# An output stage's half-size products 2 and 4 made of seven small products each, with shared sums on GpSimd and the row sums of q moved

## The chip, the cores and the metric

One core of one Trainium2 chip runs the kernel. The metric is the device time of one execution in microseconds, lower is better. The time before is 257.67 us, the median of 3 runs (257.42 to 258.0).

## The reference

Linear attention over 8 batches of 8 heads, 576 rows and 64 columns, then a two-layer network with an exact GELU over all 4608 rows.

```python
def _attn_ref(q, k, v):
    q_s = exp(q - max(q, -1)); q_s = q_s / (sum(q_s, -1) + 1e-09)
    k_s = exp(k - max(k, 2));  k_s = k_s / (sum(k_s, 2) + 1e-09)
    kv = einsum('bhsd,bhse->bhde', k_s, v)
    return einsum('bhsd,bhde->bhse', q_s, kv)
# x = attn_out as (4608, 512); w_in (512, 2048); w_out (2048, 512)
h = x @ w_in
g = 0.5 * h * (1.0 + erf(h / sqrt(2)))
return g @ w_out
```

## The kernel before, in words

The rows are handled in nine **chunks**: chunk c = 0 to 7 is 512 rows of batch c, chunk 8 is the 64 rows that each batch has left over. Every chunk goes through four stages. The attention of a batch b is `exp_q` and `exp_k` on ScalarE (ACT), row sums and reciprocal of q on VectorE (DVE; `q_sums`, lines 258 to 264), the scaling of q on GpSimd (POOL; `q_scale_parts`, line 278, eight pieces of 128x256), a cast of v on POOL (line 190), a transposing DMA of q issued by SyncE (SP; `xbar_step`, line 333), the small products k by v on TensorE (PE; `kv_mm`, line 225) and their normalization on DVE (`kv_norm`, lines 245 and 246). The x stage (`x_all`, lines 353, 380 and 378) makes the transposed attention output: eight products of 64x512, four copies out of PSUM, two by ACT and two by DVE.

The two large products use a **seven-product scheme** (Winograd's form of Strassen) on 2x2 blocks, from chunk 2 on in both. In the h stage (`h_waves`, x by w_in) the products are `mm(1..7, q)` at line 498, each quarter q four matmuls of 128x256. Sums of x blocks come from `x_sums` (DVE, line 430); products are summed in PSUM and with DVE adds `e_sum` and `r_sum`, and GELU is by ACT (line 522). `mm(7, 0)` writes a bank that `e_sum(0)` reads, so it waits for that sum; `mm(4, q)` waits for `r_sum(q)`. `s_parts` (DVE, line 430) makes the sums of g that the output stage needs.

In the y stage (`y_phase`, g by w_out) each of the seven half-size products is sixteen matmuls of 128x256 at line 686: two row blocks j, eight k tiles. Their order is 1, 5, 6, 2, 7, 3, 4. Between them stand the hooks `after(i)`, to which the loop at lines 1060 to 1078 hangs the attention of batch nb = c + 2: exp_q after product 1, exp_k and the cast of v after 5, row sums and scaling of q and the next loads after 6, and, after 3, `next_x`: the x stage of chunk c + 1, the transposing DMA of q, the k by v products of batch nb (nb below 8 only) and the first x sums. So product 4 of y stands on PE behind the x stage and the k by v products, and ahead of the h stage of the next chunk.

The order of the work is written out by hand: each engine takes its instructions in the order of the program text, waits are for semaphores, and PSUM's eight banks are handed round by the table `roles`. Before the cast of v a one-element POOL copy (`touch_s`, line 1047) waits for the last DVE sum of g.

Of the kernel before, what the change touches and what calls it, by code (L numbers as in the profile page):

```python
# [16 lines left out]
def kernel(  # L17
# [11 lines left out]
    nc = tc.nc  # L29
# [78 lines left out]
    def v_buf(b):  # L108

        i = b % 2 if b < 4 else 0  # L110
        return f32in.tile([128, HP, NS * D], FP32, tag=f"vf{i}", name="f", bufs=1)

    def load_pair(b, name, t, parts=1):
        f = v_buf(b) if name == "v" else f32in.tile([128, HP, NS * D], FP32, tag=name + "f")
        st[b][name + "f"] = f
        src = t[b].rearrange("h (p n) d -> (h p) (n d)", n=NS).rearrange("(x q) f -> q x f", q=128)
        n = HP // parts
        for i in range(parts):
            h0 = i * n
            if b == 0 and name == "k" and i == 0:  # L120

                nc.scalar.dma_start(out=f[:, 0, :], in_=src[:, 0, :])
                h0 = 1
            nc.sync.dma_start(out=f[:, h0:(i + 1) * n, :], in_=src[:, h0:(i + 1) * n, :])

    def load_k1(i):

        if i == 0:
            st[1]["kf"] = f32in.tile([128, HP, NS * D], FP32, tag="kf", name="f")
        src = k[1].rearrange("h (p n) d -> (h p) (n d)", n=NS).rearrange("(x q) f -> q x f", q=128)  # L130
        nc.sync.dma_start(out=st[1]["kf"][:, 2 * i:2 * i + 2, :], in_=src[:, 2 * i:2 * i + 2, :])

    def load_v1(i):

        if i == 0:
            st[1]["vf"] = v_buf(1)
# [321 lines left out]
    def turn_roles():  # L458
# [2 lines left out]
        roles.update(bb=r["x3"], ba=r["kv1"], x0=r["bb"], x1=r["kv0"], x2=r["x0"], x3=r["ba"],  # L461
                     kv0=r["x1"], kv1=r["x2"])

    def h_waves(c, mid):


# [45 lines left out]
        def e_sum(q):  # L512
            tt(held["B", q], held["A", q], held["r", q])
# [4 lines left out]
        def gelu(kind, *qs):  # L518
            up, half = {"C": (1, lo), "B": (1, hi), "A": (0, lo), "r": (0, hi)}[kind]
            for q in qs:  # L520
                t = 2 * q + (0 if up else HK)
                nc.scalar.activation(out=g[:, t:t + 2, half], in_=held[kind, q], func=AF.Gelu)  # L522

        vcopy, scopy = nc.vector.tensor_copy, nc.scalar.copy
        mm(1, 0, 1)
        seed(0)
        if mid:
            seed(1)
            mm(1, 2, 3)
# [36 lines left out]
        else:  # L566
            mm(5, 0, 1)
            seed(1)
            p5_copy(0, scopy)
            p5_copy(1, scopy)  # L570
            mm(6, 0, 1)
            x_sums(c, (3,))
            e_sum(0)
            e_sum(1)
            x_sums(c, (4,))
            mm(2, 0, 1)
            gelu("C", 0, 1)
# [12 lines left out]
            seed(3)  # L590
            gelu("A", 0, 1)
            p5_copy(2, vcopy)
# [66 lines left out]
    def y_operands(c):  # L659
# [8 lines left out]
        }  # L668
        return act, wgt

    def y_phase(c, ins):
# [8 lines left out]
        def two(ps):  # L680
            return ps.rearrange("p (j n) -> p j n", j=2)

        def mm(m, ps, first):
            for j in range(2):
                for k in range(HK):
                    nc.tensor.matmul(  # L686
                        ps[:, j * HN:(j + 1) * HN], act[m][:, k, j * 128:(j + 1) * 128],
                        wgt[m][:, k, :], start=(first and k == 0 and j == 0),
                        stop=(k == HK - 1), skip_group_check=True,
                    )  # L690

        def after(i):
            for fn in ins.get(i, []):
                fn()

        mm(1, pa, True)
        (nc.vector.tensor_copy if c == 1 else nc.scalar.copy)(out=c11, in_=two(pa))
        after(1)
        mm(5, pb, True)
        nc.vector.tensor_copy(out=c22, in_=two(pb))  # L700
        after(5)
        mm(6, pa, False)
        tt(two(pb), two(pa), c22)
        after(6)
        mm(2, pc, True)
        tt(c11, c11, two(pc))
        after(2)
        mm(7, pa, False)
        tt(c22, two(pa), c22)
        after(7)  # L710
        mm(3, pb, False)
        nc.scalar.copy(out=c12, in_=two(pb))  # L712
        y_store(c, 0, ysb[0])
        after(3)
        mm(4, pa, False)
        nc.scalar.copy(out=c21, in_=two(pa))
        y_store(c, 1, ysb[1])
        after(4)

    def y_last(c):  # L720
# [26 lines left out]
        for j in range(2):  # L747
# [267 lines left out]
    for m in (3, 2, 4, 1):  # L1015
# [11 lines left out]

    y_phase(1, {
        1: [sums[3], lambda: norm_q(2, 0, 2)],
        6: [lambda: norm_q(2, 1, 2, nc.vector), lambda: cast_v_all(3), lambda: xbar_step(2), lambda: exp_q(3)],  # L1030
        2: [lambda: kv_step(2), lambda: exp_k(3)],
        7: [lambda: q_sums(3)],
        3: [lambda: table(AF.Gelu)],
# [8 lines left out]
        q_scale(3, nc.gpsimd)  # L1042
        xbar_step(3)

    def touch_s():

        nc.gpsimd.tensor_copy(out=scr[:, 2:3], in_=s12[:, HK - 1, HT:HT + 1])
# [61 lines left out]
```

## Time and profile before

| what | value |
|---|---|
| median of 3 runs | 257.67 us |
| profiled execution, its own time | 257.79 us |
| its span | 255.7 us |
| granted TensorE clock | 0.998 |
| PE busy | 248.6 us, 97% of the span |
| DVE busy, ACT busy | 189.8 us and 189.1 us, 74% each |
| POOL busy | 53.9 us, 21% |
| h stage of chunk 6 | 176.6 to 188.9 us, PE busy all of it |
| y stage of chunk 6 | 188.9 to 201.75 us, PE busy all of it |

The page is read from the shares of busy time to the chain of work that ended last, and then stage by stage in the timeline: for each engine a start, a duration, and in brackets the idle time before with what ended it. Durations of matmuls overlap, so the spacing of a group is its length less one duration, divided by one less than its count. Names in the timeline are output, arrow, inputs.

### The profile page before, as it was taken

How to read it: one execution, taken by the hardware profiler on the slowest of the kernel's cores; microseconds unless marked ns; L12 is line 12 of the kernel's file. 1: busy time of each engine (PE TensorE's matmuls, PEld its weight loads, DVE VectorE, ACT ScalarE, POOL GpSimd, SP SyncE). 2: the span in 40 equal slices, each digit the busy share in tenths (PEclk: the TensorE clock that was granted, in tenths of full speed). 3: DMA queues.
4: the chain of work that ended last, by engine and by line, in shares of the span. 5: the costliest groups of instructions: out<-in, count | busy, mean ns of one | idle time of the engine just before them, and what ended most of it. 6: DMA issues, size and time to landing. Idle time of an engine off the chain costs nothing.

```text
span 255.7 us, 6526 instructions
## 1 busy us (share of the span) xinstructions
PE 248.6 (97%) x2678; PEld 195.8 (77%) x2678; DVE 189.8 (74%) x337; ACT 189.1 (74%) x323; POOL 53.9 (21%) x85
## 2 busy tenths in 40 slices
PE   7899999999999999999999999999999999999993
PEld 3444444448888888888888888888888888888883
DVE  1878698877987985898589858985798689448931
ACT  4776878699887986899688968895887687068711
POOL 1530023000705065005500560056000700000000
PEclk9999999999999999999999999999999999999999
DMA  7999999994289997933693369203400240040033
GB/s 239 401 363 424 402 408 398 399 410 178 53 256 380 267 355 234 318 143 102 228 313 142 91 222 245 45 0 118 133 3 0 103 145 3 0 167 3 0 82 86
DMA packets 43166, 50.23 MB, mean 196 GB/s; under 512 B 20224, under 2 KB 30464, under 8 KB 42880
## 3 DMA queue, kind: packets, MB, share of 16 engines
q1 hardware_dynamic: 42416, 49.13, 56.5%
q10 hardware_dynamic: 720, 0.69, 1.1%
q8 instruction: 21, 0.34, 0.5%
q14 instruction: 9, 0.07, 0.1%
HBM read 36.70 MB, written 9.44 MB: 180 GB/s over the span
## 4 chain that ended last, share of the span: by engine, by line
PE 79%; DMA 16%; DVE 1%; issue 1%; ACT 1%; ACTq 0%; SPq 0%
PE ya L686 19%; PE qa L498 19%; PE yb L686 9%; PE qb L498 9%; DMA w<-in_moe_w_in_dram 6%; PE ps L387 6%; DMA f<-in_k_dram 5%; PE qc L498 5%; PE yc L686 5%; DMA f<-in_v_dram 3%; PE ya L739 2%; DMA touch<-in_moe_w_in_dram 2%; PE yb L739 1%; PE kv L225 1%; PE ps L353 1%; DVE s L430 1%
## 5 line engine op out<-in xcount | busy, mean ns | idle before, releaser
L498 PEld LDWEIGHTS <-quad_s 128*128 128x128 bf16 x448 | 43.8, 98 | 5.2
L686 PEld LDWEIGHTS <-g 128*128 128x128 bf16 x448 | 43.2, 98 | 6.0 <-issue 0.4
L686 PEld LDWEIGHTS <-s 128*128 128x128 bf16 x336 | 32.8, 98 | 4.2 <-DVE s L430 0.4
L498 PEld LDWEIGHTS <-wi_bf 128*128 128x128 bf16 x336 | 32.9, 98 | 4.0 <-issue 0.2
L278 POOL TENSOR_TENSOR e<-e,recq 128x256 bf16<-128x256 bf16 x40 | 24.2, 642 | 30.7 <-DVE recq L264 21.1
L498 PE MATMUL qa<-quad_t,quad_s 128*128 128x256 bf16 x224 | 29.2, 273 | 0.0
L430 DVE TENSOR_TENSOR qb<-qa,r 128x512 f32<-128x512 f32 x28 | 18.2, 695 | 14.2 <-PE qa L498 9.6
L387 PE MATMUL ps<-xT,wi_bf 128*128 128x512 bf16 x128 | 28.1, 379 | 0.2 <-ACT xT L380 0.2
L686 PE MATMUL yb<-wo_bf,s 128*128 128x256 bf16 x224 | 26.9, 273 | 0.1
L686 PE MATMUL ya<-w,g 128*128 128x256 bf16 x224 | 26.8, 273 | 0.0
L263 DVE TENSOR_REDUCE qsum<-e 128x16 f32<-128x1024 bf16 (+1 forms) x12 | 20.9, 1740 | 4.6 <-ACT e L173 4.5
L387 PEld LDWEIGHTS <-wi_bf 128*128 128x128 bf16 x128 | 12.4, 98 | 15.3 <-issue 0.7
L393 ACT ACTIVATE g<-ps 128x512 bf16<-128x512 f32 x32 | 17.6, 602 | 6.2 <-PE ps L387 5.8
L173 ACT ACTIVATE e<-f 128x512 bf16<-128x512 f32 (+1 forms) x42 | 20.5, 557 | 2.0 <-DMA f<-in_q_dram 1.9
L522 ACT ACTIVATE g<-r 128x512 bf16<-128x512 f32 x28 | 17.3, 631 | 6.1 <-DVE r L430 6.1
L522 ACT ACTIVATE g<-qc 128x512 bf16<-128x512 f32 x28 | 15.2, 594 | 7.5 <-PE qc L498 7.5
L269 POOL TENSOR_TENSOR e<-e,recq 128x1024 bf16<-128x1024 bf16 (+1 forms) x4 | 9.3, 2330 | 48.5 <-DVE recq L264 41.9
L430 DVE TENSOR_TENSOR r<-qa,r 128x512 f32<-128x512 f32 x28 | 18.0, 683 | 0.9 <-PE qa L498 0.7
L178 ACT ACTIVATE ek<-f 128x2304 bf16<-128x2304 f32 (+1 forms) x10 | 17.2, 1726 | 1.1 <-DMA f<-in_k_dram 1.1
L190 POOL CAST v_aug<-f 128x576 bf16<-128x576 f32 x25 | 17.0, 716 | 3.6 <-DMA f<-in_v_dram 3.5
L378 DVE CAST xT<-ps 128x512 bf16<-128x512 f32 x18 | 11.6, 682 | 8.0 <-PE ps L353 6.4
L712 ACT COPY y_sb<-yb 128x512 f32<-128x512 f32 x7 | 4.1, 585 | 17.2 <-PE yb L686 16.1
(96 smaller groups left out, 442.0 us busy)
## 6 DMA issues: line engine op xcount, KB each, us to landing
out_dram<-y_sb SPq DMA_DIRECT2D x16, 512.0 KB, 3.4
f<-in_k_dram SPq DMA_DIRECT2D x6, 1152.0 KB, 9.6
f<-in_v_dram SPq DMA_DIRECT2D x6, 1152.0 KB, 9.2
f<-in_q_dram SPq DMA_DIRECT2D x6, 1024.0 KB, 7.0
w<-in_moe_w_in_dram SPq DMA_DIRECT2D x6, 512.0 KB, 9.0
f<-in_v_dram SPq DMA_DIRECT2D x8, 288.0 KB, 6.5
f<-in_q_dram SPq DMA_DIRECT2D x4, 512.0 KB, 8.9
w<-in_moe_w_out_dram SPq DMA_DIRECT2D x2, 1024.0 KB, 11.5
```

The source lines that it names most:

```text
L173: nc.scalar.activation(out=dst[:, i], in_=src[:, u], func=AF.Exp)
L178: nc.scalar.activation(out=ek[b % 2][:, i:i + n], in_=st[b]["kf"][:, i:i + n].rearrange("p x (n d) -> p x n d", n=NS), func=AF.Exp,)
L190: eng.tensor_copy(out=o, in_=i)
L263: nc.vector.reduce_sum(out=qsum, in_=st[b]["eq"][:, :, i * w:(i + 1) * w, :], axis=AX.X)
L278: nc.gpsimd.tensor_tensor(out=e, in0=e, op=ALU.mult, in1=st[b]["recq"][:, j, i:i + 4].unsqueeze(2).to_broadcast([128, 4, D]),)
L378: nc.vector.tensor_copy(out=st[b]["xT"][:, hp, :], in_=ps)
L387: nc.tensor.matmul(ps, wi_bf[:, dm, t * 128:(t + 1) * 128], st[c]["xT"][:, dm, :], start=(dm == 0), stop=(dm == NDM - 1),)
L393: nc.scalar.activation(out=st[c]["g"][:, t, :], in_=ps, func=AF.Gelu)
L430: eng.tensor_tensor(out=out, in0=in0, in1=in1, op=op)
L498: nc.tensor.matmul(held[kind, q][:, u], w, mov[m][:, k], start=(m in (1, 5) and u == 0 and k == 0), stop=(k == 1), skip_group_check=True,)
L522: nc.scalar.activation(out=g[:, t:t + 2, half], in_=held[kind, q], func=AF.Gelu)
L686: nc.tensor.matmul(ps[:, j * HN:(j + 1) * HN], act[m][:, k, j * 128:(j + 1) * 128], wgt[m][:, k, :], start=(first and k == 0 and j == 0), ...
```

## The change

In chunks 2 to 7 the half-size products 2 and 4 of the y stage are each computed by a second level of the same scheme: seven **sets** of four matmuls of 128x128 in place of sixteen matmuls of 128x256. A class `Two` holds it. Its weight sums are made once, on POOL, in y of chunk 1 (`two_begin`, eight operations of 128x512). Its sums of g are made in every chunk on POOL (`inner(0)` and `inner(1)` in `h_waves`, eight operations of 128x256 each: s1, s2, s4, s3 for product 4, then the same for product 2). The results are gathered in a bank X (sets 2, 3, 4, 5 side by side) and a bank D (sets 1, 6, 7 on top of each other, read in between), and added to the output tile by DVE in five adds: a, b (128x128, from D), c (128x256, D read twice), d (128x128, from X), e (128x512, from X).

The PE order of y becomes 1, 5, 6; sets 1, 5, 2, 4, 6, 3 of product 2; 7; set 7 of product 2, set 1 of product 4; the first half of 3; sets 5, 2, 6; the second half of 3; sets 7, 3; `next_x`; set 4. The copy of the first part of c21 moves from behind product 4 to behind product 7.

The row sums of q (in two halves), reciprocal, scaling and transposing DMA move from y of chunk c for batch c + 2 into h of chunk c for batch c + 1 (`q_wide`; from chunk 3 on). `touch_s` is gone. k gets the same buffers as v: two up to batch 3, and one from batch 4 on. The two buffers that this frees hold the weight sums and the sums of g. In `y_last` one copy goes from ACT to DVE.

```diff
+    def q_wide(b):
+        qsum = small.tile([128, J, H], FP32, tag="qsum")
...
+        def part(j):
+            js = slice(2 * j, 2 * j + 2)
+            nc.vector.reduce_sum(out=qsum[:, js], in_=st[b]["eq"][:, js], axis=AX.X)
+        def rest():
+            nc.vector.reciprocal(st[b]["recq"], qsum)
+            q_scale_parts(b)
+            xbar_step(b)
...
+        def inner(a):
+            if c < B:
+                two[4].sums(c, a)
+                two[2].sums(c, a)
...
             gelu("A", 0, 1)
+            inner(0)
...
             x_sums(c, (3,))
+            q_ops = q_wide(c + 1) if c + 1 <= B else []
+            for fn in q_ops[0:1]:
+                fn()
             e_sum(0)
             e_sum(1)
...
             r_sum(0)
             r_sum(1)
+            for fn in q_ops[1:]:
+                fn()
...
         gelu("A", 2, 3)
+        inner(1)
...
+        def sums(self, c, a):
+            ks = slice(2 * a, 2 * a + 2)
+            (a11, a21), (a12, a22) = self.halves(y_operands(c)[0][self.m], ks)
+            s1, s2, s3, s4 = (self.s[:, i, ks] for i in range(4))
+            tt(s1, a21, a22, eng=nc.gpsimd)
+            for o, i0, i1 in ((s2, s1, a11), (s4, a12, s2), (s3, a11, a21)):
+                tt(o, i0, i1, ALU.subtract, eng=nc.gpsimd)
...
+                        1: (A[:, e, lo], W[:, e, lo], "D", 0),
+                        2: (A[:, o, lo], W[:, o, lo], "X", 0),
+                        3: (s[:, 3, i], W[:, o, hi], "X", 1),
+                        4: (A[:, o, hi], w[:, 3, i], "X", 2),
+                        5: (s[:, 0, i], w[:, 0, i], "X", 3),
+                        6: (s[:, 1, i], w[:, 1, i], "D", 0),
+                        7: (s[:, 2, i], w[:, 2, i], "D", 0),
...
+            t2.begin(c, pc, bank(roles["x1"], "yd"))
+            t2.mm(1, 5, 2, 4)
+            t2.add("a", c11)
+            t2.mm(6, 3)
+            t2.add("b", c11)
+            after(2)
+            mm(7, pa, False)
+            tt(c22, halves(pa), c22)
+            t2.mm(7)
+            after(7)
+            nc.scalar.copy(out=c21, in_=halves(pa))
+            t4.begin(c, bank(at["ya"], "yf"), bank(roles["kv1"], "ye"))
+            t4.mm(1)
+            t2.add("c", c11)
+            mm(3, pb, False, (0,))
+            t4.add("a", c21)
+            t2.add("de", c11)
+            t4.mm(5, 2, 6)
+            t4.add("b", c21)
+            mm(3, pb, False, (1,))
+            nc.scalar.copy(out=c12, in_=halves(pb))
+            y_store(c, 0, ysb[0])
+            t4.mm(7, 3)
+            t4.add("c", c21)
+            after(3)
+            t4.mm(4)
+            t4.add("de", c21)
...
-            nc.scalar.copy(out=c12, in_=pb)
+            (nc.vector.tensor_copy if j else nc.scalar.copy)(out=c12, in_=pb)
...
-            yi[6] = [lambda: q_sums(nb), lambda: q_scale_parts(nb)]
+            yi[6] = []
-            yi[5] = [lambda: exp_k(nb), touch_s, lambda: cast_v_all(nb)]
+            yi[5] = [lambda: exp_k(nb), lambda: cast_v_all(nb)]
-        if nb <= B:
-            xbar_step(nb)
```

More of the change, by code (lines that the diff above doesn't have):

```diff
@@ L106, in load_main, with kv_buf @@
             nc.sync.dma_start(out=f[:, i * n:(i + 1) * n, :], in_=src[:, i * n:(i + 1) * n, :])
-    def v_buf(b):
+    def kv_buf(b, name):
         i = b % 2 if b < 4 else 0
-        return f32in.tile([128, HP, NS * D], FP32, tag=f"vf{i}", name="f", bufs=1)
+        return f32in.tile([128, HP, NS * D], FP32, tag=f"{name}f{i}", name="f", bufs=1)
     def load_pair(b, name, t, parts=1):
-        f = v_buf(b) if name == "v" else f32in.tile([128, HP, NS * D], FP32, tag=name + "f")
+        f = kv_buf(b, name)
         st[b][name + "f"] = f
@@ L128, in load_k1 @@
         if i == 0:
-            st[1]["kf"] = f32in.tile([128, HP, NS * D], FP32, tag="kf", name="f")
+            st[1]["kf"] = kv_buf(1, "k")
         src = k[1].rearrange("h (p n) d -> (h p) (n d)", n=NS).rearrange("(x q) f -> q x f", q=128)
@@ L462, in turn_roles @@
                      kv0=r["x1"], kv1=r["x2"])
+    def q_wide(b):
+        qsum = small.tile([128, J, H], FP32, tag="qsum")
+        st[b]["recq"] = small.tile([128, J, H], FP32, tag="recq", name="recq")
+        def part(j):
[5 more added lines that the diff above has]
+            xbar_step(b)
+        return [lambda: part(0), lambda: part(1), rest]
     def h_waves(c, mid):
@@ L591, in h_waves @@
             gelu("A", 0, 1)
+            inner(0)
             p5_copy(2, vcopy)
@@ L669, in y_operands, with __init__, halves, weights @@
         return act, wgt
+    class Two:
+        def __init__(self, m, w, s):
+            self.m, self.w, self.s = m, w, s
+        def halves(self, t, ks):
+            return [[t[:, b + 2 * ks.start:2 * ks.stop:2, n:n + 128] for n in (0, 128)] for b in range(2)]
+        def weights(self):
+            (b11, b12), (b21, b22) = self.halves(self.raw_w(), slice(0, 4))
+            t1, t2, t3, t4 = (self.w[:, i] for i in range(4))
+            for o, i0, i1 in ((t1, b12, b11), (t2, b22, t1), (t3, b22, b12), (t4, b21, t2)):
+                tt(o, i0, i1, ALU.subtract, eng=nc.gpsimd)
+        def raw_w(self):
+            return {2: wo_bf[:, DN, 0:HN], 4: w7}[self.m]
+        def sums(self, c, a):
[4 more added lines that the diff above has]
+            for o, i0, i1 in ((s2, s1, a11), (s4, a12, s2), (s3, a11, a21)):
+                tt(o, i0, i1, ALU.subtract, eng=nc.gpsimd)
+        def begin(self, c, X, D):
+            self.A, self.W = y_operands(c)[0][self.m], self.raw_w()
+            self.X, self.D = X, D
+            self.begun = set()
+        def mm(self, *sets):
+            lo, hi = slice(0, 128), slice(128, 256)
+            A, W, w, s = self.A, self.W, self.w, self.s
+            for m in sets:
+                for i in range(4):
+                    e, o = 2 * i, 2 * i + 1
+                    lhs, rhs, at, r = {
+                        1: (A[:, e, lo], W[:, e, lo], "D", 0),
[5 more added lines that the diff above has]
+                        7: (s[:, 2, i], w[:, 2, i], "D", 0),
+                    }[m]
+                    first = at not in self.begun
+                    self.begun.add(at)
+                    nc.tensor.matmul(
+                        getattr(self, at)[:, r * 128:(r + 1) * 128], lhs, rhs,
+                        start=first, stop=(i == 3), skip_group_check=True,
+                    )
+        def add(self, what, out):
+            X = self.X.rearrange("p (j n m) -> p j n m", j=2, n=2)
+            u = self.D[:, 0:128]
+            o = out.rearrange("p j (n m) -> p j n m", n=2)
+            for i in what:
+                t, x = {
+                    "a": (o[:, 0, 0], u), "b": (o[:, 0, 1], u),
+                    "c": (o[:, 1], u.unsqueeze(1).to_broadcast([128, 2, 128])),
+                    "d": (o[:, 0, 1], X[:, 1, 1]), "e": (o, X),
+                }[i]
+                tt(t, t, x)
@@ L671, in y_phase, with two_begin @@
+    def two_begin():
+        w = f32in.tile([128, 9, 512], BF16, tag="vf1", name="two_w", bufs=1)
+        s = f32in.tile([128, 9, 512], BF16, tag="kf1", name="two_s", bufs=1)
+        for i, m in enumerate((2, 4)):
+            o = slice(4 * i, 4 * i + 4)
+            two[m] = Two(m, *(t[:, o].rearrange("p x (i n) -> p x i n", i=4) for t in (w, s)))
+            two[m].weights()
+    two = {}
     def y_phase(c, ins):
@@ L678, in y_phase, with halves, mm @@
         c21, c22 = ysb[1][:, :, 0:HN], ysb[1][:, :, HN:DM]
-        def two(ps):
+        def halves(ps):
             return ps.rearrange("p (j n) -> p j n", j=2)
-        def mm(m, ps, first):
-            for j in range(2):
+        def mm(m, ps, first, js=(0, 1)):
+            for j in js:
                 for k in range(HK):
@@ L1029 @@
         1: [sums[3], lambda: norm_q(2, 0, 2)],
[L1030 removed]
+        6: [lambda: norm_q(2, 1, 2, nc.vector), lambda: cast_v_all(3), two_begin, lambda: xbar_step(2), lambda: exp_q(3)],
         2: [lambda: kv_step(2), lambda: exp_k(3)],
```

38 lines of the change are left out of this document (20 added, 18 removed).

## Prediction

> **What bounds the kernel now.** I read the shares of busy time first (PE 97% of the span), then the chain that ended last (PE 79%; the rest is nearly all the loads at the start), then the windows of single stages, where PE is busy for the whole window from h of chunk 3 on. So the kernel is bound by matmuls, and the question is what cover each one gives to the other engines. For that the timeline around the end of y of chunk 5:
>
> ```profile
> 171.82 1.91 PE L686 MATMUL yb<-wo_bf,s 128*128 128x256 bf16 x16
> ...
> 173.66 0.63 PE L353 MATMUL ps<-qT,kvc 64*64 64x512 bf16 x8
> ...
> 174.11 0.81 PE L225 MATMUL kv<-v_aug,ek 64*64 64x65 bf16 x72
> 174.15 1.29 DVE L378 CAST xT<-ps 128x512 bf16<-128x512 f32 x2 [1.16 <-PE ps L353]
> ...
> 174.85 1.92 PE L686 MATMUL ya<-w,g 128*128 128x256 bf16 x16
> 175.35 0.41 DVE L430 TENSOR_TENSOR quad_t<-xT 128x512 bf16<-128x512 bf16 x1
> ...
> 176.61 1.04 PE L498 MATMUL qa<-xT,wi_bf 128*128 128x256 bf16 x8
> ...
> 179.06 1.48 DVE L430 TENSOR_TENSOR qb<-qa,r 128x512 f32<-128x512 f32 x2 [1.64 <-PE qa L498]
> ...
> 180.10 1.09 PE L498 MATMUL qa<-quad_t,quad_s 128*128 128x256 bf16 x8
> ```
>
> PE starts its 16 matmuls 1.75 us apart per product (109 ns each). Call X the moment when it is through with product 3: 171.82 + 1.75 = 173.57. The last group shown is product 7 of h for quarters 0 and 1, at X + 6.53; it has to wait for the DVE sums at 179.06 (e_sum), ends 0.05 late for that, and is issued by X + 7.46. DVE had 1.64 us idle before them. Two rows price what is new:
>
> ```profile
> 250.59 1.06 PE L739 MATMUL yd<-w,g 128*128 128x128 bf16 x16
> ```
>
> ```profile
> L278 POOL TENSOR_TENSOR e<-e,recq x40: 607/612/829, 94.6 to 202.1; 128x256 bf16<-128x256 bf16 x40
> L269 POOL TENSOR_TENSOR e<-e,recq x4: 1899/1901/3619, 7.9 to 77.4; 128x1024 bf16<-128x1024 bf16 x3, 128x2048 bf16<-128x2048 bf16 x1
> ```
>
> The first gives 128-wide matmuls, each with its own weight load, a spacing of (1.06 - 0.22) / 15 = 56 ns. The second, from the rows of one tile, is min/median/max in ns of POOL operations with two inputs.
>
> **The change part by part.**
>
> *PE work.* A product of 16 x 109 = 1.75 us becomes 28 x 56 = 1.57 us: 0.18 us less, for 12 products 2.1 us. The Trainium skill (TensorE: Matmul & The Clock Gate, Back-to-back issue gap) states about 81 ns as the sustained spacing of pairs of weight load and matmul at 128 columns. By that a product would take 2.27 us, and the twelve would cost 6.3 us instead of saving 2.1; the 56 ns row speaks against it here.
>
> *Where that work stands.* All of product 4 stood behind X. Now six of its sets (6 x 4 x 56 ns = 1.34 us) are ahead of X and one (0.22) behind. From the start of y (call it Y) to X, PE has 10.48 - 1.75 + 1.57 + 1.34 = 11.65 us of work, 1.17 more. From X to the next Y it has 1.52 us less.
>
> *The 1.52 us are not got.* After X, DVE has a chain that does not shrink. From X: x copies 0.58 to 1.87, first x sum to 2.19, four operations of kv_norm to 3.0, second x sum to 3.33 (0.41, as without POOL beside it), then the two adds d and e of product 4 that the change puts here (0.29 as the 128x128 row of yd in the tail, 0.69 as 128x512 from PSUM) to 4.24, third x sum to 4.57, the first half of the row sums of q (1.2 us, row of 128x16 from 128x1024) to 5.7, and e_sum(0) to 6.34, e_sum(1) to 6.95. Product 7 of h can be issued at 6.41 and 7.02 and is through at X + 7.46, just as before; PE idles in front of it for the 1.5 us. Behind it the second half of the row sums (1.2) and the reciprocal (0.35) use up DVE's 0.47, 0.18 and 0.5 us of idle time in the rest of h and cost about 0.1. Per chunk: 0.1.
>
> *Stalls in y without POOL.* Add a must read D between sets 1 and 6; it queues behind the DVE sum after product 6 (0.69): done 6.42 us after Y instead of the 6.2 at which set 6 is due, with the handover of 0.07 a stall of 0.29. Product 4's set 5 overwrites the bank of product 7, which DVE reads (0.69) and ACT copies after it (0.59): set 5 waits to 1.63 us after product 7, due at 1.32: 0.31. ACT's row of exps and table loads ends about 9.65 after Y, so that copy comes a further 0.33 later if nothing else holds PE up. So a chunk costs 1.17 + 0.29 + 0.31 + 0.33 + 0.1, some 2.1 us more: X to X 27.8 where the before has 25.75 (146.23 to 171.98 in the chain).
>
> *POOL.* Its queue in chunks 3 to 7 is now: eight scalings of q, eight sums (inner(0)), eight sums (inner(1)), cast of v. It cannot begin before the reciprocal. On DVE, r_sum(1) follows product 7 of h and ends at X + 8.5, then half a row sum and the reciprocal: 10.06, POOL starts at 10.2. Eight scalings at 4.82 / 8 = 0.60 us end at 15.0, near Y. Sum 15 of 16 (s4 of product 2) is needed by set 3 of product 2. No row shows POOL adding two bf16 tiles. From below: a cast with one input, 128x256, 1.47 us for four (0.37 each). From above: the slowest scaling, 0.83. Nearest is the 128x256 scaling, same size and two inputs, 0.60, which I take. Then s4 is ready at 10.2 + 4.83 + 15 x 0.604 = X + 24.1, set 3 ends at 24.3, and product 7 (1.75) and what follows it up to x (3.63 with its stall) bring the next X to 29.7: 3.9 us more than 25.75 and 1.9 more than without POOL. The point from which POOL decides is 0.47 us a sum. What contention adds to DVE's sums of g late in h lies inside that wait.
>
> *Chunk by chunk.* y of chunk 2 (no scaling in its h, sums from 83.4 on, when GELU r is done): s4 at Y + 7.06 against Y = 85.40; 1.17 + 0.29 + 0.31 + 0.35 = 2.1. X of chunk 2 to X of chunk 6: four times 3.93. Chunk 6 to 7 has no kv products (reciprocal at 9.4, X to X 29.0 against 25.1): 3.9. h of chunk 8 has no row sums: there product 7 of h is through at X + 5.8 instead of 6.9, a gain of 1.1. In the tail the copy on DVE lets ACT issue its last two stores sooner (its copy sat behind 0.99 us of issuing): 0.4 gained. **Sum: 2.1 + 15.7 + 3.9 - 1.1 - 0.4 = 20.2.**
>
> *Costed at nothing.* two_begin: eight operations of 0.18 + 512 x 1.68 ns = 1.04 us follow the casts that end at 68.8, so POOL is free at 77.2, where its next work begins today; if late, x of chunk 3 has 15 us of cover. The transposing DMA (1.8 us issue, 3.8 to landing) waits on SP for POOL, to X + 15, and is needed at X + 29.7; the loads behind it wait for exp_k and for the casts (about X + 27), land in 9.6 and are used a chunk later; the stores behind these are due at X + 29. The k load's single buffer: same cover.
>
> The sum against the profiled execution's 257.79 (span 255.7 and 2.1 around it; the median of the runs is 0.12 less) gives **278.0**.
>
> **Rivals.**
>
> *POOL adds faster than the scaling row* (0.47 or less, towards the 0.37 of the cast). Then DVE and ACT set the period at 27.8: 2.1 + 4 x 2.1 + 2.2 - 1.1 - 0.4 = 11.2, that is 269. For it: both inputs are bf16, and the scaling reads an f32 column. Against it: 1.68 ns an element, twice the slope of the casts, looks like one step per input. Chance 0.17.
>
> *POOL adds slower*, because DVE's sums of g run beside it and each sum waits for the one before. For it: the slowest scaling is 0.83, and a DVE sum beside scalings took 0.83 instead of 0.41:
>
> ```profile
> L430 DVE TENSOR_TENSOR quad_t<-xT x14: 411/414/829, 73.4 to 227.2; 128x512 bf16<-128x512 bf16 x14
> ```
>
> Against it: those eight scalings took 4.97 together, not 4.82. Each 0.1 us costs 6 x 15 x 0.1 = 9 us, so 0.70 gives 287. Chance 0.20. The Trainium skill (GPSIMD Engine Reference, section 3.1) has a two-input add of 2048 fp32 columns at 4497 ns, where the row here has 3619. An estimate by that page is 0.74 us a sum and about 290.
>
> *PE alone decides*, the other side: if everything added stays hidden, 2.1 us are gained: 255.7. That needs sums below 0.37 us, and DVE's chain from X to e_sum(0) 1.4 us shorter than its rows add up to, so that it ends by X + 4.9. Nothing in the trace points there but the 1.64 us of idle time, which d, e and the half row sum (2.1) exceed. Chance 0.06.
>
> **How the numbers follow.** Forecast (POOL sets the period at 0.53 to 0.66 us a sum, 271 to 283): 0.55; faster POOL 0.17; slower POOL 0.20; PE alone 0.06; 0.02 for no difference. The range takes the faster POOL whole (267.5) and the slower one up to 0.71 us a sum (288); it leaves out its tail and the faster side, under 0.2. Faster by over 0.2%, about what a measurement of this kernel can tell: 0.06; within 0.2%: 0.02; slower: 0.92.
>
> **What would show it.** 128-wide matmuls at 56 ns. Eight scalings of 0.60 just ahead of y, sixteen POOL sums of about 0.6 back to back to about 9 us into y, and PE's weight loads of product 2's sums idle some 2 us for POOL; about 1.5 us of PE idle in front of product 7 of h for e_sum. X to X 29.7. I am wrong if POOL's sums end before set 5 is due, or if PE goes through the start of h without idling.

## The result and the profile after

The changed kernel takes **311.45 us** (median of 4 runs, 311.04 to 311.6), beside 257.68 us for the kernel before: a ratio of 1.2084, interval [1.2063, 1.2104]. The profiled execution took 311.59 us, its span is 309.8. The prediction of 278.0 (267.5 to 288.0) had the direction, and not the size: 33 us are missing in it.

The page of the changed kernel, busy time per engine, then the granted clock in 40 slices, then the chain that ended last:

```profile
PE 267.1 (86%) x2816; PEld 204.8 (66%) x2822; DVE 225.0 (73%) x397; ACT 190.3 (61%) x322; POOL 143.5 (46%) x185
...
PEclk9999999999998999869995999979996899969999
...
PE 48%; POOL 30%; DVE 11%; issue 4%; DMA 3%; ACT 2%; SPq 0%; POOLq 0%; DVEq 0%
POOL two_s L430 22%; PE ps L387 9%; POOL e L278 8%; PE qa L514 8%; PE ya L795 7%; PE qb L514 5%; PE ps L664 4%; PE yb L795 3%; PE yc L750 3%; DVE y_sb L430 2%; DMA f<-in_v_dram 2%; PE ya L879 2%; DVE quad_t L430 2%; PE yf L750 2%; DMA f<-in_q_dram 1%
```

The clock row of before:

```profile
PEclk9999999999999999999999999999999999999999
```

PE, 97% busy before, is 86% busy. In the chain POOL has 30% of the span, with two entries: the sums for the small products (two_s, 22%) and the scalings of q (8%). And the clock row dips in each of the chunks 2 to 7, which the row of before does not (mean granted clock 0.945 for 0.998). The waits of PE (total us, times, longest) say which instruction stood for whom:

```profile
PE yc L750 <- POOL two_s L430: 25.6, 7, 4.9
PE qa L514 <- DVE qb L430: 4.4, 5, 0.9
PE yb L795 <- DVE s L430: 3.7, 6, 2.0
```

Only 34 us of waits for 54 us of loss, so the rest has to be looked for in durations. The timeline from x of chunk 6 to product 7 of its y (start, us; in brackets the idle time before) answers to the one shown of before; X, as the prediction counts it, is 174.75 here:

```profile
174.85 0.63 PE L353 MATMUL ps<-qT,kvc 64*64 64x512 bf16 x8
...
179.27 1.21 DVE L471 TENSOR_REDUCE qsum<-e 128x16 f32<-128x1024 bf16 x1
...
180.40 1.29 DVE L430 TENSOR_TENSOR qb<-qa,r 128x512 f32<-128x512 f32 x2
181.14 1.20 PE L514 MATMUL qa<-quad_t,quad_s 128*128 128x256 bf16 x8 [0.92 <-DVE qb L430]
...
184.86 5.51 POOL L278 TENSOR_TENSOR e<-e,recq 128x256 bf16<-128x256 bf16 x8 [13.84 <-ACT g L538]
...
190.33 1.11 POOL L430 TENSOR_TENSOR two_s<-g 128x256 bf16<-128x256 bf16 x1
...
190.84 1.15 DVE L430 TENSOR_TENSOR s<-g,s 128x1024 bf16<-128x1024 bf16 x1
...
196.41 0.27 PE L750 MATMUL yc<-two_w,two_s 128*128 128x128 bf16 x2
...
196.90 0.67 POOL L430 TENSOR_TENSOR two_s<-g,two_s 128x256 bf16<-128x256 bf16 x1
...
201.63 0.40 PE L750 MATMUL yc<-two_w,two_s 128*128 128x128 bf16 x2 [4.94 <-POOL two_s L430]
...
203.52 2.48 PE L795 MATMUL ya<-w,g 128*128 128x256 bf16 x16
```

Before, DVE had 1.64 us idle in front of e_sum and product 7 of h hardly waited. Now the row sums of q stand there, e_sum starts at X + 5.65 and product 7 at X + 6.39, after 0.92 us idle. Then POOL: eight scalings from X + 10.1, the first sum at X + 15.6. The first six sums take 190.33 to 196.82, 1.08 us from start to end each on average, the next nine 196.90 to 203.07, 0.69 each. The change of pace falls where DVE's own sums of g (190.84 and its neighbours) end. PE stands 4.94 us inside set 5 of product 2 (two of its four matmuls ran at 196.41, the other two need a sum from `inner(1)`), and what it does after that is slow: product 7 at 203.52 takes 2.48 us for 1.91 before. The windows (length; busy time and count of PE, PEld, DVE, ACT, POOL; granted clock, DMA share, GB/s) show it:

```profile
196.20:201.60 5.40, 0.49 (x8) 0.31 (x5) 1.58 (x4) 3.84 (x4) 5.14 (x8) 0.97 0.53 119
201.60:205.80 4.20, 4.17 (x34) 3.75 (x35) 0.29 (x1) 0.00 (x0) 4.07 (x7) 0.63 0.01 4
```

In the window that follows the wait the granted clock is 0.63, and sets are 0.43 us apart instead of 0.22.

The sum of the loss, from the starts of the x stage (96.29, then 224.58 in the last of six, before; 103.95 and 280.22 after): 7.7 us up to x of chunk 3, 48.0 in the five periods between (35.77, 35.13, 34.63, 35.81, 34.93 for 25.81, 25.80, 25.76, 25.81, 25.11), and 1.5 gained behind them. That is 54.1, the difference of the spans.

### The profile page after: what moved, and what is told of

It is laid out like the page before. It is cut to its first block, busy times and chain, and to the rows that moved or that the text cites. A ratio compares the mean times of both kernels' runs of the same rounds, so it can differ in the third digit from the quotient of the medians.

```text
span 309.8 us, 6990 instructions
## 1 busy us (share of the span) xinstructions
PE 267.1 (86%) x2816; PEld 204.8 (66%) x2822; DVE 225.0 (73%) x397; ACT 190.3 (61%) x322; POOL 143.5 (46%) x185
## 4 chain that ended last, share of the span: by engine, by line
PE 48%; POOL 30%; DVE 11%; issue 4%; DMA 3%; ACT 2%; SPq 0%; POOLq 0%; DVEq 0%
POOL two_s L430 22%; PE ps L387 9%; POOL e L278 8%; PE qa L514 8%; PE ya L795 7%; PE qb L514 5%; PE ps L664 4%; PE yb L795 3%; PE yc L750 3%; DVE y_sb L430 2%; DMA f<-in_v_dram 2%; PE ya L879 2%; DVE quad_t L430 2%; PE yf L750 2%; DMA f<-in_q_dram 1%
## 5 line engine op out<-in xcount | busy, mean ns | idle before, releaser
L278 POOL TENSOR_TENSOR e<-e,recq 128x256 bf16<-128x256 bf16 x40 | 27.6, 723 | 70.6 <-ACT g L538 70.6
L430 POOL TENSOR_TENSOR two_s<-g 128x256 bf16<-128x256 bf16 x48 | 39.8, 845 | 2.3 <-ACT g L538 2.3
L838 ACT COPY y_sb<-ya 128x512 f32<-128x512 f32 x6 | 3.5, 586 | 51.0 <-DVE y_sb L430 51.0
L750 PEld LDWEIGHTS <-two_s 128*128 128x128 bf16 x192 | 15.5, 112 | 28.5 <-POOL two_s L430 26.8
L795 PE MATMUL yb<-wo_bf,s 128*128 128x256 bf16 x224 | 29.2, 276 | 3.7 <-DVE s L430 3.7
L795 PEld LDWEIGHTS <-g 128*128 128x128 bf16 x256 | 28.1, 111 | 6.1 <-ACT g L393 0.2
L387 PE MATMUL ps<-xT,wi_bf 128*128 128x512 bf16 x124 | 27.8, 379 | 0.2
L430 DVE TENSOR_TENSOR y_sb<-y_sb,yd 128x128 f32<-128x128 f32 (+1 forms) x20 | 6.4, 322 | 28.3 <-PE yd L750 28.1
L750 PE MATMUL yc<-two_w,two_s 128*128 128x128 bf16 x24 | 3.9, 254 | 25.2 <-POOL two_s L430 25.2
L795 PE MATMUL ya<-w,g 128*128 128x256 bf16 x128 | 21.8, 344 | 0.0
L430 POOL TENSOR_TENSOR two_s<-two_s,g 128x256 bf16<-128x256 bf16 x24 | 20.0, 834 | 1.9
## 6 DMA issues: line engine op xcount, KB each, us to landing
f<-in_v_dram SPq DMA_DIRECT2D x8, 288.0 KB, 6.7
```

The source lines that it names most:

```text
L278: nc.gpsimd.tensor_tensor(out=e, in0=e, op=ALU.mult, in1=st[b]["recq"][:, j, i:i + 4].unsqueeze(2).to_broadcast([128, 4, D]),)
L387: nc.tensor.matmul(ps, wi_bf[:, dm, t * 128:(t + 1) * 128], st[c]["xT"][:, dm, :], start=(dm == 0), stop=(dm == NDM - 1),)
L430: eng.tensor_tensor(out=out, in0=in0, in1=in1, op=op)
L750: nc.tensor.matmul(getattr(self, at)[:, r * 128:(r + 1) * 128], lhs, rhs, start=first, stop=(i == 3), skip_group_check=True,)
L795: nc.tensor.matmul(ps[:, j * HN:(j + 1) * HN], act[m][:, k, j * 128:(j + 1) * 128], wgt[m][:, k, :], start=(first and k == 0 and j == 0), ...
```

## The experiments

The theory after the result: POOL's queue, scalings and then sums, sets the period; POOL and DVE lengthen each other when both add tiles that lie in SBUF; PE's long wait for POOL lowers its clock; and apart from all that the cover behind X is lost. Rivals: PE or DVE alone (the lost cover, the new adds) explain most of it; the sums on POOL are slow by themselves; the slow clock only shows the wait and costs nothing; the small products are a loss in any place. All ratios are to the kernel before, run on the same chip.

**Without POOL's sums (e1_no_sums).** The sums are left out; sets 3, 5, 6 and 7 take plain blocks of g in their place.

```diff
         def inner(a):
-            if c < B:
-                two[4].sums(c, a)
-                two[2].sums(c, a)
+            return
...
-                        5: (s[:, 0, i], w[:, 0, i], "X", 3),
+                        5: (A[:, e, hi], w[:, 0, i], "X", 3),
```

> The changed kernel without GpSimd's sixteen sums of g per chunk: sets 3, 5, 6 and 7 take plain blocks of g in place of the sums, so the output leaves them out. All matmuls, DVE adds and the moved q work stay. Theory (GpSimd's sums set the period, at 0.69 us alone and 1.09 us beside DVE's sums of g): the no-GpSimd price of the prediction is left, X to X 27.8 us and about 269 us in all (266 to 272), PE clock 1.0 throughout, DVE's sums of g back at 0.60 to 0.70 us. Rival (the small matmuls, their adds or the order of y cost most): 290 us or more.

Measured: 273.61 us, 1.0619 [1.0596, 1.0643], a little above. No wait for POOL, granted clock 0.998, periods 28.45, 28.73, 28.55 and 28.02. Its waits of PE:

```profile
PE qa L514 <- DVE qb L430: 4.4, 5, 0.9
PE yb L793 <- DVE s L430: 2.5, 4, 1.5
```

The wait for e_sum (qb) is the same 4.4 us as with POOL's sums. So 16 of the 54 us remain without POOL's sums, and 38 come with them. Of the 16, 4.1 lie ahead of x of chunk 3 (100.41 for 96.29).

**Without DVE's sums of g in h (e2_no_dve_sums).** DVE's eight `s_parts` operations per chunk are left out of h, so y reads stale sums; POOL's queue is untouched.

```diff
             r_sum(3)
-            s_parts(c, 0, 4, (1,))
...
-        s_parts(c, 0, 4, (2, 3, 4) if mid else (3, 4))
-        s_parts(c, 4, 4, (1, 2, 3, 4))
```

> The changed kernel without DVE's eight sums of g in the h stage of chunks 2 to 8 (the y stage reads the sums that chunk 1 left, so these are left out of the output). GpSimd's work is the same. Theory (a GpSimd sum and a DVE sum of two SBUF tiles lengthen each other): all sixteen sums at 0.67 to 0.70 us, scalings back at 0.60, X to X shorter by 0.64 + 6 x 0.40 = 3.0 us at least, some 290 to 296 us in all. Rival (the long sums come from ACT writing g, or from one sum waiting for the one before): sums stay at 1.0 to 1.1 us near the start of y, and the time falls by less than 5 us.

Measured: 286.23 us, 1.1145 [1.1081, 1.1208]: 25 us less than the changed kernel, more than I expected. The rows of the tile two_s (min/median/max in ns), first of the changed kernel:

```profile
L430 POOL TENSOR_TENSOR two_s<-g x48: 667/670/1120, 84.9 to 272.9; 128x256 bf16<-128x256 bf16 x48
```

and then without DVE's sums:

```profile
L430 POOL TENSOR_TENSOR two_s<-g x48: 665/669/677, 84.4 to 247.8; 128x256 bf16<-128x256 bf16 x48
```

Without DVE's sums a POOL sum is 0.67 us, 0.68 at most; with them the longest is 1.12. ACT writes g in both runs, so ACT is not the cause. The other side of it is DVE's row by form (busy us, mean ns), before:

```profile
L430 DVE TENSOR_TENSOR s<-g,s 128x1024 bf16<-128x1024 bf16 x14 | 9.6, 683 | 0.0
```

and after:

```profile
L430 DVE TENSOR_TENSOR s<-g,s 128x1024 bf16<-128x1024 bf16 x14 | 15.2, 1087 | 0.0
```

So each takes from the other. Scalings are 614 ns without DVE's sums, 723 with them. The Trainium skill (SBUF — State Buffer, Who interferes with whom) says that a DVE instruction with two inputs in SBUF contends with a GpSimd instruction that reads SBUF, and the trace agrees: in the changed kernel DVE's adds with one input in PSUM keep their time beside POOL's scalings (1.34 and 1.28 us for two, 1.29 for two ahead of the scalings). The experiment also shortens DVE's queue, and some of the 25 us are that: PE's waits for s (3.7) go too. So does most of the low clock (mean 0.987), which the next experiment prices.

**Work to fill the wait (e3_filler).** Forty more matmuls of 128x256, whose results are overwritten, stand in front of product 2's sets from chunk 3 on: 40 x 109 ns = 4.4 us of extra work per chunk.

```diff
             t2.begin(c, pc, bank(roles["x1"], "yd"))
+            for i in range(40 if c > 2 else 0):
+                nc.tensor.matmul(
+                    pc[:, 0:HN], act[2][:, i % HK, 0:128], wgt[2][:, i % HK, :],
+                    start=True, stop=True, skip_group_check=True,
+                )
```

> The changed kernel with forty more matmuls of 128x256 (4.4 us) in chunks 3 to 7, ahead of product 2's sets, into a bank that set 5 clears: work with no use, in the time in which PE waits for GpSimd. Theory (the wait of 4.9 us lets the clock fall, and product 7 and the sets after the wait run at half of it): granted clock 1.0, product 7 back to 1.75 us from 2.3 to 3.0, the sets to 0.22; the kernel with more work is 4 to 7 us faster than the changed one, 304 to 308 us. Rival (the slow matmuls come from something else, such as reads beside GpSimd): 311 us or more.

Measured: 304.34 us, 1.1809 [1.1786, 1.1832]: 7 us less time with 22 us more work. The periods are 33.8, the last 33.2, on average 1.6 less than the 35.25 of the changed kernel, and the clock row has lost its dips but for one around chunk 2, which has no filler:

```profile
PEclk9999999999999899999999999999999999999999
```

So the low clock was no mere sign: filling the wait gave back 7 us of the 54. The periods agree one by one. From set 3 of product 2 to the first half of product 3 the changed kernel takes 4.47, 3.68, 3.19, 4.62 and 4.10 us in the chunks 3 to 7, where the spacings at full clock make 2.41; that is 8.0 us too much. The filler's periods are 1.98, 1.34, 0.82, 2.03 and 1.76 us shorter, 7.9 in all (its x of chunk 3 comes 0.9 later).

The Trainium skill (TensorE: Matmul & The Clock Gate, What's actually happening) states that the array's clock halves after an idle window of some 3.4 us. For the five waits of 4.9 us the trace agrees: each was followed by sets 0.43 us apart. But here a shorter wait can do it too. In chunk 2 of the changed kernel a wait of 1.99 us was followed by 4.73 us at a granted clock of 0.64:

```profile
91.18 1.95 PE L795 MATMUL yb<-wo_bf,s 128*128 128x256 bf16 x12 [1.99 <-DVE s L430]
...
92.92 3.15 PE L795 MATMUL ya<-w,s 128*128 128x256 bf16 x16
```

In the filler's chunk 2 the same matmuls, behind the same wait, ran at full clock:

```profile
90.72 1.48 PE L795 MATMUL yb<-wo_bf,s 128*128 128x256 bf16 x12 [1.99 <-DVE s L430]
...
92.04 1.91 PE L795 MATMUL ya<-w,s 128*128 128x256 bf16 x16
```

What decides for a wait of 2 us no run shows. Mostly such waits did little: with waits of at most 2.7 us (without DVE's sums) the mean granted clock was 0.987, with waits of at most 2.2 us (below, q back in y) 0.994.

**The move of q alone (e4_q_only).** The kernel before with `q_wide` in h, and nothing else of the change.

```diff
+            q_ops = q_wide(c + 1) if c + 1 <= B else []
...
-            yi[6] = [lambda: q_sums(nb), lambda: q_scale_parts(nb)]
+            yi[6] = []
```

> The kernel before with only the move of q's row sums, scaling and transposing DMA from y into h. Theory (DVE's idle time ahead of e_sum takes the first half row sum, the rest costs about 0.1 a chunk, and GpSimd has nothing that waits behind the scaling): 257 to 259 us. Rival (the move itself costs, by DVE's later sums or the transposing DMA): 262 us or more.

Measured: 259.69 us, 1.0078 [1.0059, 1.0097], above what I expected: 26.2 a period for 25.8. Product 7 of h does not wait, DVE still has idle time in front of e_sum, since the adds d and e are not there. What is lost is later in h: the scalings run beside DVE's first sums of g (1.04 us for 0.68), so r_sum comes late and product 4 of h waits for it. 2 us, then, for the move by itself.

**Product 4 alone (f3_prod4_only) and product 2 alone (f2_prod2_only).** Product 2, or product 4, is whole again; q stays in h.

```diff
-            t2.mm(1, 5, 2, 4)
-            t2.add("a", c11)
-            t2.mm(6, 3)
-            t2.add("b", c11)
+            mm(2, pc, True)
+            tt(c11, c11, halves(pc))
```

> The changed kernel with small products for product 4 alone; product 2 is whole; q's work stays in h. GpSimd has eight sums a chunk, needed later than product 2's. Theory (lost cover): X to X is longer by the 1.34 us of sets ahead of X, 0.3 to 0.6 of waits for the bank of product 7, and 0.4 from q's scaling beside DVE's sums; nothing is got back behind X: some 267 to 271 us, with a wait of about 0.9 us for e_sum in every h. Rival (the cover is not needed): 258 to 261 us.

Measured: 275.4 us, 1.069 [1.0657, 1.0723], above the range; the periods are 28.47. PE's waits:

```profile
PE qa L514 <- DVE qb L430: 4.4, 5, 0.9
PE yb L794 <- DVE s L430: 3.7, 6, 2.0
PE yf L749 <- ACT y_sb L833: 1.8, 6, 0.3
```

The wait for e_sum and the one for ACT's copy of product 7's bank are there without product 2: they belong to product 4, which no longer stands behind X. (The e_sum wait needs the row sums of q in h as well: it is gone when either is taken away, below.) ACT's copy holds set 5 up for 0.30 a chunk, where the prediction adds 0.31 and 0.33. What the expectation left out is the wait for s, in each y: 3.7 of the 4.4 us above its range.

```diff
-            t4.begin(c, bank(at["ya"], "yf"), bank(roles["kv1"], "ye"))
-            t4.mm(1)
...
-            t4.mm(4)
-            t4.add("de", c21)
+            mm(4, pa, False)
```

> The changed kernel with small products for product 2 alone; product 4 is whole again and stands behind the x stage; q's work stays in h. Theory: the cover behind X is back, so no wait for e_sum; GpSimd has eight sums of g fewer a chunk and its queue ends about 0.5 us after PE would need it: some 260 to 266 us. Rival (the wait for GpSimd is not a matter of the length of its queue): 285 us or more.

Measured: 269.89 us, 1.0491 [1.047, 1.0512], above the range: the expectation held neither add a's stall (0.72 here, 0.29 in the prediction) nor the wait for s. But the wait for e_sum is gone, and so is every wait for POOL:

```profile
PE yd L749 <- DVE y_sb L430: 4.3, 6, 0.7
PE yb L794 <- DVE s L430: 3.9, 6, 2.2
```

With q's work in h, each product alone costs 12 to 18 us and both together 54, because only together do their sums reach the point from which POOL decides.

**q back in y (f4_q_back).** The change with row sums, scaling and transposing DMA of q back in y, behind product 2's sets. POOL's sixteen sums then begin as soon as their g is there.

```diff
-            for fn in q_ops[1:]:
-                fn()
...
+        if nb <= B:
+            xbar_step(nb)
...
+            yi[2] = [lambda: q_sums(nb), lambda: q_scale_parts(nb)]
```

> The changed kernel with q's row sums, scaling and transposing DMA back in y, behind set 3 of product 2. GpSimd starts its sums of g when the GELUs allow, near X + 12 instead of X + 15.6, and DVE has no half row sum ahead of e_sum. Theory: PE's wait for GpSimd shrinks from 4.9 to about 2 us, the clock stays at 1.0, the wait for e_sum goes; X to X shorter by 4 to 6 us: 280 to 290 us. Rival (q's scaling in front is not what makes the sums late): 300 us or more.

Measured: 275.86 us, 1.0713 [1.0697, 1.0729], better than I expected: periods of 28.19.

```profile
PE yc L745 <- POOL two_s L430: 8.0, 11, 2.2
```

25.6 us of waiting for POOL are down to 8.0, no wait exceeds 2.2 us, the clock is 0.994 (one dip is left, in chunk 2 behind the wait of 2.2), and e_sum holds nothing up. Taking q's work out of h, the 5.5 us of scalings in front of POOL's sums and the row sums on DVE, is worth 35.6 us, 7 a chunk: with it go the long wait, the low clock behind it and the e_sum stall. How much is due to the scalings and how much to the row sums was not tried singly.

**Product 2 alone with q in y and POOL's last sums behind DVE's (f1_prod2_calm).** A first try at a version without the losses.

```diff
-        inner(1)
         s_parts(c, 0, 4, (2, 3, 4) if mid else (3, 4))
         s_parts(c, 4, 4, (1, 2, 3, 4))
+        nc.gpsimd.tensor_copy(out=scr[:, 2:3], in_=s12[:, HK - 1, HT:HT + 1])
+        inner(1)
...
+            t2.mm(1)
+            t2.add("a", c11)
         mm(6, pa, False)
...
+            mm(7, pa, False)
+            after(7)
+            t2.mm(5, 2, 4, 6, 3)
```

> An attempt at a version that beats both: only product 2 is made of small products, product 4 stays whole as the cover behind the x stage, q's work stays in y as in the kernel before, and GpSimd's last four sums of g start only when DVE's sums of g are done. PE order 1, 5, set 1, 6, 7, sets 5, 2, 4, 6, 3, then 3, set 7. Theory (the small matmuls save 0.18 us a product at 56 ns, and the harm is GpSimd's queue, its contention and the lost cover): no wait for GpSimd, no wait for e_sum, 6 x 0.18 = 1.1 us gained less some 0.5 for DVE's fuller end of y: 256.6 to 257.7 us. Rival (small products cost by themselves): 259 us or more.

Measured: 268.15 us, 1.0412 [1.0396, 1.0427], a clear miss, with periods of 27.1.

```profile
PE ya L790 <- DVE yb L430: 4.7, 6, 0.8
PE yb L790 <- DVE s L430: 1.7, 1, 1.7
...
PE ps L353 <- DVE y_sb L430: 0.9, 5, 0.2
```

POOL and e_sum hold up nothing; my own order does. With the small sets moved behind it, product 7 comes right behind product 6 and overwrites the bank that the sum after 6 still reads: 0.8 in every y. The x stage waits for add c, which reads one of its banks: its first product starts 0.58 us ahead of the others, and some 0.5 of that is lost.

```profile
181.77 0.40 PE L353 MATMUL ps<-qT,kvc 64*64 64x512 bf16 x1
...
182.35 0.62 PE L353 MATMUL ps<-qT,kvc 64*64 64x512 bf16 x7 [0.18 <-DVE y_sb L430]
```

And 3.8 us are lost ahead of x of chunk 3 (100.05 for 96.29). Of these, 1.4 lie ahead of y of chunk 2 (86.80 for 85.40), where the weight sums run on POOL while DVE makes chunk 2's x sums.

**Product 2 alone, in better order (g1_prod2_tuned, g2_prod2_qlater).** From chunk 3 on, with weight sums in h of chunk 3, sets 5, 2, 4, 6, 3 between products 6 and 7, and D in a bank of kv. The second has q's sums behind the adds instead of ahead of them.

```diff
-            t2.begin(c, pc, bank(roles["x1"], "yd"))
+            t2.begin(c, pc, bank(roles["kv1"], "yd"))
...
-            mm(7, pa, False)
-            after(7)
             t2.mm(5, 2, 4, 6, 3)
-            after(2)
             t2.add("bde", c11)
+            after(2)
+            mm(7, pa, False)
             tt(c22, halves(pa), c22)
+            after(7)
             mm(3, pb, False)
             t2.mm(7)
```

> Only product 2 is made of seven small products, from chunk 3 on (chunk 2 plain), with its weight sums taken by POOL in h of chunk 3; its POOL sums in h stand behind DVE's, q's sums and scaling are in y as before the change. PE's order in y is 1, 5, set 1, 6, sets 5 2 4 6 3, product 7, product 3, set 7, the x products, 4; the second bank is the one that kv uses, not the one that x_all writes. Theory (the small products cost only their count, and the losses were the queue of POOL, the clock and banks read late): one saving of 0.18 us in each of five chunks, 256.6 to 257.4 us, X to X near 25.6, no wait of PE for POOL. Rival (adds on DVE behind q's sums hold set 7 or the x products): 258 to 262 us with a wait of PE for DVE of 0.3 us or more in each y.

> The same with q's sums on DVE (2.28 us) behind the three adds that follow set 3, not ahead of them, so q's scaling on POOL starts some 3 us later. Theory: the adds are no longer late, 256.6 to 257.4 us; if the rival holds for the kernel with q's sums ahead, this one is faster than that one. Other rival: the later scaling holds the sums of q's part or the transposes in h, 258 to 260 us with PE waiting in h.

Measured: 257.15 us, 0.9973 [0.9962, 0.9984], and 257.62 us, 0.9996 [0.9987, 1.0005]. The second is above its range, with periods of 26.15. The adds b, d and e are no longer late, but now the sum after product 7 and add c stand behind q's sums, and the k by v products wait for add c:

```profile
PE kv L225 <- DVE y_sb L430: 1.3, 3, 0.4
```

No wait of PE for the later scalings shows.

The first is inside its range, but its periods (25.57, 25.85, 26.07, 26.00, 24.94) show no steady gain: PE waits 0.3 for add e in front of the x stage and 0.3 for add c in front of the k by v products. Where its 0.7 us come from is the question of the next two.

**The same without small products (h1_no_products), and with the adds placed anew (g3_prod2_banks).**

```diff
-        if c > 2:
+        if c > 99:
             t2 = two[2]
```

> The kernel of the run before last (product 2 small from chunk 3 on, q's sums ahead) with its small products taken out again: every half-size product whole, so that only the side edits are left, k's double buffers, the one-element copy moved into h and one tail copy on DVE. If the 0.7 us that kernel gained come from the five small products (0.18 us each), this one takes 257.7 to 258.0 us like the kernel before. If they come from the side edits (its x stage of chunk 3 starts 0.34 us earlier than before, its tail is 0.2 us shorter, and its X to X of 25.57 to 26.07 shows no gain), this one takes 257.0 to 257.3 us.

Measured: 257.35 us, 0.9986 [0.9976, 0.9996], between the two: its periods are those of before to 0.01 us, and 0.3 us come from the side edits. So the small products of the first kernel in better order bring hardly more than 0.3 us in all (0.9973 beside 0.9986, intervals that overlap): their waits eat the rest.

```diff
-            t2.mm(5, 2, 4, 6, 3)
-            t2.add("bde", c11)
+            t2.mm(6)
+            t2.add("b", c11)
+            after(6)
+            t2.mm(5, 2, 4, 3)
+            t2.add("de", c11)
             mm(7, pa, False)
-            tt(c22, halves(pa), c22)
             after(7)
+            t2.mm(7)
+            t2.add("c", c11)
+            tt(c22, halves(pa), c22)
             mm(3, pb, False)
-            t2.mm(7)
```

> The kernel with product 2 small from chunk 3 on, its adds placed anew: set 6 first and add b right behind the sum after product 6, ahead of q's sums; d, e and c behind them, and the last sum with product 7 after that; set 7 right behind product 7. That takes away two waits of 0.3 us (x_all for add e, kv for add c). If the small products save their 0.18 us once nothing waits, X to X is 25.6 us in each chunk and the time 256.2 to 256.8 us. If DVE's adds only move the wait elsewhere, X to X stays at 25.8 to 26.1 and the time at 257.0 to 257.5 us.

Measured: **256.02 us, 0.9934 [0.9922, 0.9945]**, slightly better than I expected, and 0.7% faster than the kernel before. Its timeline of y of chunk 5:

```profile
168.01 0.39 PE L747 MATMUL yd<-two_w,two_s 128*128 128x128 bf16 x4
168.24 0.39 PE L747 MATMUL yc<-two_w,two_s 128*128 128x128 bf16 x4
...
169.13 1.91 PE L792 MATMUL ya<-w,g 128*128 128x256 bf16 x16
170.88 0.39 PE L747 MATMUL yd<-two_w,two_s 128*128 128x128 bf16 x4
171.10 1.91 PE L792 MATMUL yb<-wo_bf,s 128*128 128x256 bf16 x16
172.94 0.63 PE L353 MATMUL ps<-qT,kvc 64*64 64x512 bf16 x8
```

Five sets between products 6 and 7 take 1.12 us, set 7 0.22, and nothing is idle. The periods are 25.57, 25.57, 25.57, 25.62 and 25.15. Against the kernel without small products it is 1.33 us less, 1.1 in the profiled spans. Of that, 0.80 lie in the five periods: four gain 0.18 to 0.24 each, and the last gains nothing (25.15 for 25.11). There no k by v products stand behind the x stage, and product 4 of chunk 6 waits for the late sum after product 7, which reads its bank:

```profile
PE ya L792 <- DVE y_sb L430: 0.2, 1, 0.2
```

The other 0.25 lie behind the last matmul, and small products do not explain them.

## Why the prediction was wrong

*Right.* The spacing of 56 ns: sets at 0.22 us wherever the clock is full, and a saving of about 0.2 us a product once nothing waits (0.18 predicted; 0.18 to 0.24 in four periods of the last kernel). The lost cover: e_sum was forecast to let product 7 of h go at X + 6.41 and it went at X + 6.39; 1.5 us of idle time were forecast there, and from the starts of the groups it is 1.4 (1.09 in front of product 7 by a spacing of 109 ns, 0.27 in front of the second group of h). That POOL sets the period, and its start (X + 10.1, 10.2 forecast). Chunk 8 and the tail: 1.5 us gained, as forecast. The period without POOL: 27.8 forecast, 28.0 to 28.7 in the run without POOL's sums, which has q's scalings beside DVE's sums in it. There some luck is in it: the 0.33 for a late copy by ACT did not show, while add a's stall was 0.72 for 0.29 with product 2 alone, and waits for s of 0.3 a chunk were not foreseen.

*The step that failed* is the price of a POOL sum, and the sentence that what contention adds to DVE's sums of g "lies inside that wait". I took 0.604 us from the scaling row. Alone a sum takes 0.67 (without DVE's sums), which is 1.0 us over fifteen; beside DVE's sums it takes about 1.08 from start to end, and over the fifteen to s4 of product 2 it came to 0.85. In the chunk of the timeline the sums took 12.74 us for 9.06: +3.7. The scalings took 5.51 for 4.83: +0.7. DVE's sums are not covered by POOL's queue, they lengthen it, and are lengthened: two queues that the prediction added up one beside the other share something. I had the rival in hand, with the row that showed it (a DVE sum of 0.83 us beside scalings instead of 0.41), and weighed it down because those eight scalings had taken 4.97 and not 4.82. There three short DVE sums (0.48, 0.65 and 0.83 us) had met the last of eight scalings; here long DVE sums in a row meet the scalings and the first six sums. At the price that the rival gave (9 us for each 0.1 us), 0.85 instead of 0.604 makes 300.

*Two terms were missing.* The clock stands nowhere in the prediction: I had counted a PE wait of some 2 us, and did not ask what a longer one would do. Behind the wait of 4.94 us, from set 3 of product 2 to the first half of product 3, it cost 0.8 in this chunk, and 8.0 over the chunks 3 to 7; filling the wait brought 7 us in all. And chunk 2: X came 7.7 us late instead of 2.1. I had costed the weight sums at nothing, as if only POOL's next work could be late. But they run beside chunk 2's x sums on DVE. The third of these, before and after:

```profile
74.89 0.42 DVE L430 TENSOR_TENSOR quad_t<-xT 128x512 bf16<-128x512 bf16 x1
```

```profile
75.15 1.37 DVE L430 TENSOR_TENSOR quad_t<-xT 128x512 bf16<-128x512 bf16 x1
```

So products of h wait, and y of chunk 2 begins 1.4 us late (86.84 for 85.40). In it product 5 waits 1.99 us for s (1.55 without POOL's sums of g), and behind that wait the low clock lengthens the rest of product 5 and product 6 by 1.7. That is some 5 of the 5.6 us beyond the forecast. Without POOL's sums of g 4.1 us remained of the 7.7, at full clock; how these divide between the weight sums and the adds of y was not tried singly.

In spans, 33.9 us are to be explained (54.1 less the forecast 20.2): 5.6 lie in chunk 2 (7.7 for 2.1), 28.4 in the five periods (48.0 for 19.6), and nothing behind. The period of the timeline is 4.9 longer than the 29.7 forecast, and its terms make 0.7 + 3.7 + 0.8, less 0.1 as POOL started earlier: 5.1. The others are up to 1.2 us longer, and that is the clock: in them, too, the sums take 12.7 us to s4, but the slow stretch behind the wait costs 1.3 to 2.2 us instead of 0.8.

*The rival on the other side*, PE alone at 255.7, has its point in another kernel than this one: it holds once the sums are ready early, the adds stand clear of the banks, and only product 2 is small. The last kernel shows it at 256.02 with five products. Product 4 small was not tried in such an order: it takes the cover from behind X, and with it alone the period was 28.47 where the move of q alone has 26.2.

## What to carry to other kernels

A queue's length is no sum of single prices where another engine adds tiles in SBUF at the same time: price such work from a row taken beside that neighbour, and ask which end of the overlap the critical instruction lies at. A wait of PE can cost more than its length: after each wait of 4.9 us the work behind ran slow (0.63 in the window shown), after a wait of 2 us it sometimes did. And a saving of 0.2 us a product is only had where every add, bank and sum around it has slack: place the adds by the bank that is wanted next, and run a kernel with nothing but the side edits beside it, or their gain is taken for that of the change.

## What the runs showed of the hardware

- A POOL add of two 128x256 bf16 tiles takes 0.67 us alone and 1.0 to 1.1 beside DVE adds of two bf16 tiles of g, which go from 0.68 to between 1.04 and 1.15 us at the same time (128x1024). DVE adds with an input in PSUM do not slow (0.69).
- Forty more matmuls in a wait of PE made the kernel 7 us faster: granted clock 0.993 for 0.945.
- Behind a wait of PE of 1.99 us the granted clock was 0.64 in one kernel (4.73 us long) and 1.00 in another; behind five waits of 4.9 us the work was slow each time.
- Pairs of weight load and matmul at 128 columns ran 56 ns apart in a whole kernel, at full clock.
